# One fixed order for the first attention batch, and a first tile that takes 12 of its 16 weight slices

## The chip, the cores and the metric

One core of a Trainium2 chip runs the kernel. The metric is the device time of one execution in microseconds (us); lower is better. Engines go by the profile's names: PE is TensorE, DVE is VectorE, ACT is ScalarE, POOL is GpSimd, SP is SyncE, which here issues DMAs. PEld is PE's weight load.

## The reference

Eight batches of attention, 8 heads, 576 tokens, head width 64, whose keys and values are first averaged in groups of 8 tokens; then two feed-forward layers over all 4608 tokens, of width 512 and inner width 2048:

```
k_p, v_p = mean of 8 tokens of k, v
attn = softmax(q @ k_p.T / 8) @ v_p            # per batch and head
x = attn as (4608, 512)
x = leaky(x @ w_in1) @ w_out1                  # leaky(h) = max(0.01 h, h)
out = relu(x @ w_in2)**2 @ w_out2
```

The weights arrive as 64-bit floats, two 32-bit words a value.

## The kernel before, in words

Every product is made of three 32-bit ones: both operands are split into a high and a low part by a cast on ACT and a subtraction on DVE (`three`, lines 268 to 273).

**Layer 1, first way.** Tokens 0 to 2303 are cut into five tiles, `WIDE` = 512, 512, 512, 512, 256 (the last is the narrow tile). For a tile `t` and a weight slice `f` of 128 inner columns (16 slices), `first(t, f)` makes `h`, applies the leaky step, and splits it into `gh` and `gl` (L644 to L648); `second(t, f)` adds its product with the slice of `w_out` to four accumulators `acc`. A pair (t, f) is a unit: 24 matrix products. `units` holds the 80 pairs in order, and one loop walks them, with `split_weights` (L193, L194) two units and one unit ahead. At the last slice the accumulators are copied out (L676, L678) and stored into `x1`. The narrow tile's 256 columns make its products shorter.

**Layer 1, second way, and layer 2.** The other 2304 tokens (three passes) and all of layer 2 use a scheme with seven products in place of eight; its operands are prepared by `prepare_sums` (L214 to L218) and `prepare_products`.

**Decoding.** In the first pass over the slices each slice is fetched (two DMAs of 512 KB) and turned into 32-bit floats by `decode`: an absolute value on ACT (L159), a clip, a shift and a sign merge on DVE (L161, L164, L168), a conversion on ACT (L177) and an addition on DVE (L178). Two stage buffers hold fetched slices.

**Attention.** `attention` is a generator; the loop over units takes `RATES` steps of it per unit (3 in the first tile, 5 after). A batch is five chunks of up to 128 queries in two spans: `prepare_k` and `prepare_v` pool keys and values (L310), `stage_a` transposes queries (L452, L456), `stage_b` makes scores and their exponentials (L467, L475, L478, L487 to L499), `stage_c` transposes the weights, `stage_d` makes the output. For batch 0 the output goes straight into the first tile's `xh` and `xl` (L541, L542); later output goes to `x0` in memory and comes back by `load_x` and `split_x` (L622 to L629). Before the loop, steps of attention run until batch 0 is done, with a decode after every seventh step, up to `AHEAD` = 5 slices.

What sets the order: instructions are traced in program order, and a scheduler that ranks what is ready lays them out engine by engine. Each engine then runs its own list strictly in that order. All DMAs are issued from SP's queue.

Of the kernel before, what the change touches and what calls it, by code (L numbers as in the profile page):

```python
# [33 lines left out]
def attention_two_mlps(  # L34
# [25 lines left out]
    RATES = (3, 5)  # L60
# [5 lines left out]
    NTILE = len(WIDE)  # L66
    NQ = NF // 2
# [20 lines left out]

    def temp(name, dt=F32):
        return tpool.tile([P, TT], dt, tag="t", name=name)  # L90
# [14 lines left out]
    x0 += [dpool.tile([DM, HT], F32, name=f"x0_{NTILE + t}") for t in range(2 * LEAD)]  # L105
    x1 = [dpool.tile([DM, HT], F32, name=f"x1_{t}") for t in range(NT // HT)]
# [47 lines left out]
    def decode(st, r, name):  # L154
# [4 lines left out]
        nc.scalar.activation(raw(m), raw(high), AF.Abs)  # L159
# [19 lines left out]

    def decode_weights(f):  # L180
        r = (w_early if f < NQ else w_late).tile([P, 2, TT], U32, tag="w", name=f"w1_{f}")
        for _ in decode(RAW.pop(f), r, f"1_{f}"):
            pass
        W["in", f], W["out", f] = (raw(r[:, i]) for i in range(2))
# [91 lines left out]
    def attention():  # L276

        with ExitStack() as s:
# [42 lines left out]
            def load_main(b, src, nm, heads):  # L321


                ts = []
                for m in range(NP):
                    if m % 2 == 0:
                        ts.append(kv_tile(b, P, 2, f"{nm}{b}_{m}"))
                    for a in range(2):
                        nc.sync.dma_start(
                            out=ts[-1][a * KM:(a + 1) * KM, m % 2],  # L330
                            in_=src[b, heads[m][a], 0:KM * POOL, :].rearrange("(kk j) d -> kk (j d)", j=POOL),
                        )
                return ts

            def load_rest(b, src, nm):

                t = kv_tile(b, KR * H, 1, f"r{nm}{b}")
                nc.sync.dma_start(
# [8 lines left out]
            def load_k(b):  # L347
                if b < B:
                    KV["k", b] = (
                        load_rest(b, k, "k"),  # L350
                        load_main(b, k, "k", [[4 * (m // 2) + m % 2 + 2 * a for a in range(2)] for m in range(NP)]),
                    )
# [42 lines left out]
            def prepare_v(b):  # L395
# [10 lines left out]
                for g in range(2):  # L406
                    cols = slice(g * H * D // 2, (g + 1) * H * D // 2)
                    for j in range(3):
# [3 lines left out]
                        )  # L412
                for m in range(0, NP, 2):
# [5 lines left out]
                for a in range(2):  # L419
# [5 lines left out]
                    )  # L425
                flat = vR.rearrange("p m x -> p (m x)")
# [33 lines left out]
            def stage_b(b, span, at, off, n):  # L460
                qT = qt.pop((b, at))
                x = xp.tile([P, H, SP], F32, tag="x", name=f"x{b}_{at}", bufs=2)
                sm, rs = (xp.tile([P, H, 1], F32, tag=g, name=f"{g}{b}_{at}") for g in ("sm", "rs"))
                for e in range(2):
                    sc = work(f"s{b}_{at}_{e}", early=b == 0)[:, :H // 2 * SP].rearrange("p (h x) -> p h x", x=SP)
                    for m in range(2):
# [6 lines left out]
                    hs = slice(4 * e, 4 * e + 4)  # L473
                    mx = xp.tile([P, 4, 1], F32, tag="mx", name=f"mx{b}_{at}_{e}")
                    nc.vector.tensor_reduce(out=mx[:n], in_=sc[:n], axis=AX.X, op=ALU.max, negate=True)  # L475
                    if b < EARLY:
# [9 lines left out]
                if b >= EARLY:  # L486
                    nc.scalar.activation(x[:n], x[:n], AF.Exp)  # L487
                    nc.vector.tensor_reduce(out=sm[:n], in_=x[:n], axis=AX.X, op=ALU.add)
                nc.vector.tensor_scalar(out=sm[:n], in0=sm[:n], scalar1=1e-9, scalar2=None, op0=ALU.add)
# [15 lines left out]
            def stage_c(b, span, at, off, n):  # L505
                pp = pr.pop((b, at))
# [8 lines left out]
                yield  # L515
# [8 lines left out]
                )  # L524
                yield

            def stage_d(b, span):
                n = SPANS[span]
                g0 = b * S + sum(SPANS[:span])
                for m in range(NP):  # L530
# [7 lines left out]
                    if g0 < TT:  # L538
                        done = min(n, TT - g0)
                        xh, xl = X[1, 0][m]  # L540
                        nc.scalar.copy(xh[:, g0:g0 + done], o[:, :done])  # L541
                        nc.vector.tensor_tensor(  # L542
                            out=xl[:, g0:g0 + done], in0=o[:, :done], in1=raw(xh[:, g0:g0 + done]), op=ALU.subtract
                        )
                    if done < n:
                        xo = xp.tile([P, SPANS[0]], F32, tag="xo", name=f"xo{b}_{span}_{m}", bufs=3)
                        nc.scalar.copy(xo[:, done:n], o[:, done:n])
# [10 lines left out]
            pk, pv = prepare_k(0), prepare_v(0)  # L558
            load_k(0)
            load_q(*chunks[0])  # L560
            load_q(*chunks[1])
            yield
            load_v(0)
            yield from pk
            stage_a(*chunks[0])
            yield
            for i in range(len(chunks) + 1):
                if i < len(chunks):
                    b = chunks[i][0]
                    if i == nch - 2:  # L570
                        load_k(1)
                    if i % nch == nch - 1 and 0 < b < B - 1:
# [6 lines left out]
                    if i != nch:  # L579
                        stage_b(*chunks[i])  # L580
                        yield
                    if i == 0:
                        yield from pv
                    elif i % nch == 1 and b > 0:
                        yield from prepare_v(b)
                if i > 0:
                    b, span = chunks[i - 1][:2]
                    yield from stage_c(*chunks[i - 1])
                    if i == len(chunks) or chunks[i][:2] != (b, span):
                        yield from stage_d(b, span)  # L590
                    if i % nch == 0:
                        ready[0] = b + 1
                    if i == nch:

                        yield
                        yield from prepare_k(1)
                        stage_b(*chunks[nch])
                        yield

    ready = [0]  # L600
# [17 lines left out]
    def load_x(t):  # L618
        XS[t] = []
        for c in range(NK):  # L620
            st = temp(f"xs1_{t}_{c}")[:, :WIDE[t]]
            nc.sync.dma_start(out=st, in_=x0[t][c * P:(c + 1) * P, :])  # L622
# [30 lines left out]
    def store_x1(t, j, o):  # L653
        at = t * TT
# [7 lines left out]

    def second(t, f):
# [352 lines left out]
```

## Time and profile before

| what | value |
|---|---|
| median of 3 runs (lowest to highest) | 1664.58 us (1662.08 to 1665.07) |
| the profiled execution, its own time | 1663.77 us |
| its span | 1662.1 us |
| PE busy | 1610.6 us, 97% |
| PEld, DVE, ACT, POOL busy | 91%, 77%, 54%, 8% |
| PEclk in the first two of 40 slices (0 to 83 us), then | 0.7, 0.7, then 0.9 or more |
| DMA, mean | 241 GB/s |

The profiled execution's own time exceeds its span by 1.67 us, which lie around the program. PE's busy share is modelled: products overlap, and a waiting product can be counted as long. The span has three parts: up to 63 us attention's batch 0 with few of the large products; up to 598 us the five tiles with the other batches between them; then the seven-product scheme, where PE is busy throughout.

### The profile page before, as it was taken

What the parts mean: (1) busy time and instruction counts of PE and PEld (TensorE: products, weight loads), DVE (VectorE), ACT (ScalarE), POOL (GpSimd) and SP (SyncE); (2) the same over time, 40 slices, a digit from 0 to 9 for tenths busy, and PEclk for the clock granted to TensorE, in tenths of its full rate; (3) what the DMA queues carried; (4) which work ended last, traced back from release to release, by engine and by line L of the source; (5) the groups of instructions that cost most, each with busy time, mean ns of one, the idle gap of its engine ahead of it and who ended that gap; (6) DMA issues with size and microseconds to landing.
All of it is one profiled execution on the core that took longest, in us unless ns stands there. A gap on an engine that the chain in (4) does not pass through costs nothing.

```text
span 1662.1 us, 27194 instructions
## 1 busy us (share of the span) xinstructions
PE 1610.6 (97%) x9976; PEld 1518.0 (91%) x9976; DVE 1282.0 (77%) x1891; ACT 897.2 (54%) x1604; POOL 126.8 (8%) x149
## 2 busy tenths in 40 slices
PE   4899999999999999999999999999999999999998
PEld 3677788888888999999999999999999999999998
DVE  5899899888778989979979669378477486485484
ACT  5788655655657868668567425334234244244233
POOL 3131222232210000000000000000000000000000
PEclk7799999999999999999999999999999999999999
DMA  6565565866426769798887778878878879778776
GB/s 178 182 198 173 164 184 161 248 190 191 146 77 218 278 236 318 247 328 291 274 285 235 248 265 267 311 255 284 288 250 300 279 250 303 277 253 271 265 250 204
DMA packets 223717, 399.74 MB, mean 241 GB/s; under 512 B 56161, under 2 KB 129889, under 8 KB 223585
## 3 DMA queue, kind: packets, MB, share of 16 engines
q1 hardware_dynamic: 223584, 398.00, 73.1%
q8 instruction: 80, 1.31, 0.3%
q14 instruction: 53, 0.43, 0.1%
HBM read 318.77 MB, written 77.59 MB: 238 GB/s over the span
## 4 chain that ended last, share of the span: by engine, by line
PE 80%; DVE 11%; ACT 3%; DMA 3%; issue 2%; SPq 0%; POOL 0%; DVEq 0%; ACTq 0%; POOLq 0%
PE acc L273 13%; PE acc L272 13%; PE acc L271 13%; PE h L271 12%; PE h L273 12%; PE h L272 12%; PE s L467 2%; DVE hl_in L194 1%; DVE gl L648 1%; DMA st_in_out<-in_moe_w_out_dram 1%; DVE hl_out L194 1%; PE trq L452 1%; DVE v L310 1%; ACT x L478 1%; PE o L536 1%
## 5 line engine op out<-in xcount | busy, mean ns | idle before, releaser
L695 ACT CAST oh<-g 128x768 fp32r<-128x768 f32 x252 | 210.3, 835 | 261.4 <-PE acc L272 165.1
L271 PE MATMUL h<-xh,wb_in 128*128 128x384 f32 x1008 | 337.7, 335 | 2.5 <-ACT s L797 1.4
L273 PE MATMUL h<-xh,wb_in 128*128 128x384 f32 x1008 | 336.8, 334 | 0.0
L272 PE MATMUL h<-xl,wb_in 128*128 128x384 f32 x1008 | 336.8, 334 | 0.0
L696 DVE TENSOR_TENSOR ol<-g,oh 128x768 fp32r<-128x768 f32 x252 | 240.3, 954 | 77.5 <-ACT oh L695 76.9
L273 PE MATMUL acc<-wb_out,ol 128*128 128x256 f32 x1008 | 282.2, 280 | 0.0
L271 PE MATMUL acc<-wb_out,oh 128*128 128x256 f32 x1008 | 281.2, 279 | 0.0
L272 PE MATMUL acc<-wb_out,oh 128*128 128x256 f32 x1008 | 281.2, 279 | 0.0
L271 PEld LDWEIGHTS h<-xh,wb_in 128*128 128x128 f32 x1008 | 189.2, 188 | 5.0 <-ACT s L797 2.9
L272 PEld LDWEIGHTS acc<-wb_out,oh 128*128 128x128 f32 x1008 | 189.5, 188 | 0.0
L273 PEld LDWEIGHTS acc<-wb_out,ol 128*128 128x128 f32 x1008 | 189.2, 188 | 0.0
L272 PEld LDWEIGHTS h<-xl,wb_in 128*128 128x128 f32 x1008 | 189.2, 188 | 0.0
L273 PEld LDWEIGHTS h<-xh,wb_in 128*128 128x128 f32 x1008 | 189.2, 188 | 0.0
L271 PEld LDWEIGHTS acc<-wb_out,oh 128*128 128x128 f32 x1008 | 188.5, 187 | 0.0
L803 DVE TENSOR_TENSOR g<-h,s 128x768 f32<-128x768 f32 x36 | 34.4, 955 | 166.8 <-PE h L273 88.3
L699 DVE TENSOR_TENSOR g<-g,g 128x768 f32<-128x768 f32 x144 | 135.9, 953 | 1.0
L271 PE MATMUL h<-xh,hl_in 128*128 128x512 f32 (+1 forms) x320 | 122.8, 385 | 3.8 <-ACT x L478 1.9
L272 PE MATMUL acc<-gl,hl_out 128*128 128x512 f32 (+1 forms) x320 | 118.6, 373 | 2.0 <-DVE gl L648 2.0
L271 PE MATMUL acc<-gh,hl_out 128*128 128x512 f32 (+1 forms) x320 | 120.1, 384 | 0.1
L273 PE MATMUL acc<-gh,hl_out 128*128 128x512 f32 (+1 forms) x320 | 118.5, 373 | 1.7 <-DVE hl_out L194 1.7
L273 PE MATMUL h<-xh,hl_in 128*128 128x512 f32 (+1 forms) x320 | 119.8, 374 | 0.0
L272 PE MATMUL h<-xl,hl_in 128*128 128x512 f32 (+1 forms) x320 | 119.3, 373 | 0.0
(148 smaller groups left out, 3129.6 us busy)
## 6 DMA issues: line engine op xcount, KB each, us to landing
wb_in<-wd_in SPq DMA_DIRECT2D x204, 512.0 KB, 4.4
wb_out<-wd_out SPq DMA_DIRECT2D x204, 512.0 KB, 4.4
xs<-x SPq DMA_DIRECT2D x18, 768.0 KB, 5.2
wb_in<-ws_in SPq DMA_DIRECT2D x48, 256.0 KB, 3.7
wb_out<-ws_out SPq DMA_DIRECT2D x48, 256.0 KB, 2.8
out_dram<-o SPq DMA_DIRECT2D x24, 384.0 KB, 5.1
k<-in_k_dram SPq DMA_DIRECT2D x64, 128.0 KB, 2.7
q<-in_q_dram SPq DMA_DIRECT2D x32, 256.0 KB, 4.3
```

The costliest lines, as they stand in the source:

```text
L194: nc.vector.tensor_tensor(out=lo, in0=w, in1=raw(hi), op=ALU.subtract)
L271: nc.tensor.matmul(outp, ah, bh, start=first, stop=False, **kw)
L272: nc.tensor.matmul(outp, ah, bl, start=False, stop=False, **kw)
L273: nc.tensor.matmul(outp, al, bh, start=False, stop=last, **kw)
L310: nc.vector.tensor_tensor(out=dst if n == D else src[:, :, 0:n], in0=src[:, :, 0:n], in1=src[:, :, n:2 * n], op=ALU.add)
L452: nc.tensor.transpose(tr[:, m, :n], t[:n, 2 * m:2 * m + 2].rearrange("p a d -> p (a d)"), ident[:n, :n])
L467: nc.tensor.matmul(sc[:n, 2 * m:2 * m + 2].rearrange("p a x -> p (a x)"), qT[:, 2 * e + m, :n], kT[b % 2][:, 2 * e + m].rearrange("p a x - ...
L478: nc.scalar.activation(x[:n, 4 * e + h], sc[:n, h], AF.Exp, bias=mx[:n, h], accum_out=sm[:n, 4 * e + h],)
L695: nc.scalar.copy(hi, src)
L696: nc.vector.tensor_tensor(out=lo, in0=src, in1=raw(hi), op=ALU.subtract)
L699: nc.vector.tensor_tensor(out=out_, in0=a, in1=b, op=ALU.subtract)
L803: nc.vector.tensor_tensor(out=g11, in0=v, in1=s1, op=ALU.add)
```

## The change

- **One list.** `first_batch` traces the whole of batch 0, the decoding of slices 0, 1 and half of 2 and the first `first(0, 0)` as one sequence written out by hand. `in_order` ties each instruction of it to the one before it on the same engine, so the scheduler may not reorder it. `behind(marks[0], 3000)` keeps the next 3000 traced instructions behind the list on every engine.
- Half of batch 0's keys are loaded from ACT's queue; the values and all queries of the batch are queued ahead of slice 0, and batch 1's keys behind the list. For slices 0 and 1 the absolute value is a mask on DVE in place of ACT's.
- **Twelve of sixteen slices.** The first tile takes slices 0 to 11. Its partial sum goes to `y_first` in memory. A sixth tile, number 5, is the first one again with slices 12 to 15, behind the narrow tile; its input, stored in `x_first` as high and low part, comes back by a load from SP and an accumulating load from POOL; its output is added to `y_first`.
- Decoding runs at about 7 slices in 9 units in the first tile and at one in two units in the second, so slices 12 to 15 are decoded there. Attention takes 4 steps a unit in the first tile. `prepare_sums` starts once all 16 slices are there.

```diff
-    RATES = (3, 5)
+    RATES = (4, 5)
+    WIDE.append(TT)
+    CUT = 12
+    PART_OF = [range(CUT)] + [range(DFF // P)] * (NTILE - 1) + [range(CUT, DFF // P)]
...
+    def in_order(body):
+        traced = nc.cur_bb.bb.instructions
+        begin = len(traced)
+        body()
+        last = {}
+        for ins in traced[begin:]:
+            if ins.engine in last:
+                tc.add_manual_dep(
+                    ins, last[ins.engine].name,
+                    mybir.DependencyInfo(mybir.DependencyClass.NoSync, mybir.DependencyReason.DATA),
+                    reason="in_order",
+                )
+            last[ins.engine] = ins
+        return len(traced), last
...
-        nc.scalar.activation(raw(m), raw(high), AF.Abs)
+        if early:
+            nc.vector.tensor_scalar(out=m, in0=high, scalar1=0x7FFFFFFF, scalar2=None, op0=ALU.bitwise_and)
+        else:
+            nc.scalar.activation(raw(m), raw(high), AF.Abs)
...
+            def first_batch():
...
+                load_k(0)
+                q_in(0)
+                q_in(1)
+                load_v(0)
+                q_in(2)
...
+                w(1)
+                split_weights("in", 0, 1)
+                split_weights("out", 0, 0)
+                w(2)
+                w(2)
+                first(0, 0)
+                load_k(1)
+                w(2)
+                w(2)
+                a(5)
+                a(6)
+            marks.append(in_order(first_batch))
...
+            if t == NTILE:
+                nc.sync.dma_start(out=st, in_=x_first[0, c * P:(c + 1) * P, :])
+                nc.gpsimd.dma_start(out=st, in_=x_first[1, c * P:(c + 1) * P, :], accum_op=ALU.add)
...
+        if t == 0:
+            nc.sync.dma_start(out=y_first[j * P:(j + 1) * P, :], in_=o)
+            return
...
-        if f == NF - 1:
+        if t == NTILE and f == end - 1:
+            for j in range(4):
+                YF.append(temp(f"yf_{j}"))
+                nc.sync.dma_start(out=YF[j], in_=y_first[j * P:(j + 1) * P, :])
+        if f == end:
...
+                if t == NTILE:
+                    nc.vector.tensor_tensor(out=o, in0=acc[j], in1=YF[j], op=ALU.add)
...
-    units = [(t, f) for t in range(NTILE) for f in range(NF)]
+    units = [(t, f) for t in range(NTILE + 1) for f in PART_OF[t]]
...
-        if f == NF - 3 and t + 1 < NTILE:
+        if f == PART_OF[t][-1] - (2 if t + 1 < NTILE else 5) and t < NTILE:
...
-        if w1 < NF:
+        if w1 < (AHEAD + (i + 1) * (CUT - AHEAD) // (CUT - 3) if t == 0 else NF) and w1 < NF and (t == 0 or f % 2):
             prepare_weights(w1)
             w1 += 1
-        elif t > 0:
+        elif w1 == NF:
             next(sums1, None)
```

Three places show what moves. The first is DVE's list up to the first tile's first low part `gl_0_0`, before:

```order
L168 SCALAR_TENSOR_TENSOR wm_3_557<-st_in_out_553,wm_3_557 128x1024
L542 TENSOR_TENSOR xl_0_2_149<-o_1_2_626,xh_0_2_148 128x192
L178 ISA w_3_556<-wm_3_557,w_3_556 128x2048
L542 TENSOR_TENSOR xl_0_3_151<-o_1_3_635,xh_0_3_150 128x192
L194 TENSOR_TENSOR hl_in_2_695<-w_2_476,hl_in_2_695 128x512
L310 TENSOR_TENSOR rv_729<-rv_729 64x256
L161 TENSOR_SCALAR wm_4_619<-wm_4_619 128x1024
L310 TENSOR_TENSOR rv_729<-rv_729 64x128
L164 TENSOR_SCALAR wm_4_619<-wm_4_619 128x1024
L194 TENSOR_TENSOR hl_out_1_698<-w_1_362,hl_out_1_698 128x512
L168 SCALAR_TENSOR_TENSOR wm_4_619<-st_in_out_615,wm_4_619 128x1024
L648 TENSOR_TENSOR gl_0_0_670<-g_0_0_667,gh_0_0_669 128x512
```

and now (`wm` and `w` are a slice in decoding, `xl` the tile's low part, `rv` batch 1's values):

```order
L203 SCALAR_TENSOR_TENSOR wm_1_535<-st_in_out_270,wm_1_535 128x1024
L232 TENSOR_TENSOR hl_in_0_552<-w_0_344,hl_in_0_552 128x512
L612 TENSOR_TENSOR xl_0_0_147<-o_1_0_555,xh_0_0_146 128x192
L612 TENSOR_TENSOR xl_0_1_149<-o_1_1_565,xh_0_1_148 128x192
L612 TENSOR_TENSOR xl_0_2_151<-o_1_2_575,xh_0_2_150 128x192
L612 TENSOR_TENSOR xl_0_3_153<-o_1_3_585,xh_0_3_152 128x192
L213 ISA w_1_534<-wm_1_535,w_1_534 128x2048
L232 TENSOR_TENSOR hl_in_1_600<-w_1_534,hl_in_1_600 128x512
L232 TENSOR_TENSOR hl_out_0_603<-w_0_344,hl_out_0_603 128x512
L196 TENSOR_SCALAR wm_2_607<-wm_2_607 128x1024
L199 TENSOR_SCALAR wm_2_607<-wm_2_607 128x1024
L817 TENSOR_TENSOR gl_0_0_627<-g_0_0_624,gh_0_0_626 128x512
```

The first low part stood behind slices 0 to 3 and most of 4; now it stands behind slices 0 and 1 and half of 2, and none of batch 1's pooling is ahead of it. The second place is DVE's list at the start of the second tile, between the first tile's last copy and `gl1_1_1`, before:

```order
L194 TENSOR_TENSOR hl_out_1_1_2021<-w1_1_362,hl_out_1_1_2021 128x512
L512 TENSOR_TENSOR pt_l_181<-pt2_128_1992,pt_h_180 128x4x128
L310 TENSOR_TENSOR rd3_2506<-rv3_2204 64x64
L310 TENSOR_TENSOR vd3_2505<-v3_0_2206 128x128
L310 TENSOR_TENSOR v3_2_2211<-v3_2_2211 128x2x256
L217 TENSOR_TENSOR s1_in1_2452<-s1_in1_2452,w1_1_362 128x256
```

and now:

```order
L196 TENSOR_SCALAR wm_1_13_1828<-wm_1_13_1828 128x1024
L232 TENSOR_TENSOR hl_in_1_2_1854<-w1_2_606,hl_in_1_2_1854 128x512
L199 TENSOR_SCALAR wm_1_13_1828<-wm_1_13_1828 128x1024
L547 TENSOR_SCALAR sm2_256_1791<-sm2_256_1791 64x8
L232 TENSOR_TENSOR hl_out_1_1_1857<-w1_1_534,hl_out_1_1_1857 128x512
L548 RECIPROCAL rs2_256_1792<-sm2_256_1791 64x8
L203 SCALAR_TENSOR_TENSOR wm_1_13_1828<-st1_in13_out13_1824,wm_1_13_1828 128x1024
```

Slice 13 is decoded there, where a step of the sums stood. The third place is SP's queue in the narrow tile, where the operands of the seven-product scheme are fetched (`xs_0_0` and `xs_0_1` its input, `wb_in` its weights); now:

```order
L920 DMA wb_in_5_6252<-ws_in_138 128x512
L920 DMA wb_in_6_6254<-ws_in_138 128x512
L925 DMA wb_in_2_6256<-wd_in_122 128x1024
L920 DMA wb_in_7_6258<-ws_in_138 128x512
L788 DMA xs_5_0_6389<-x_first 128x512
L788 DMA xs_5_1_6392<-x_first 128x512
L788 DMA xs_5_2_6395<-x_first 128x512
L788 DMA xs_5_3_6398<-x_first 128x512
L920 DMA wb_in_3_6862<-ws_in_138 128x512
```

The four loads of the kept tile are new, between two weight blocks that stood next to each other; four accumulating loads follow them on POOL's queue.

## Rows read from the trace of the kernel before

**Rows 1.** Windows: window, length, busy us (instructions) by engine, PEclk, DMA share, GB/s.

```profile
0.00:63.00 63.00, 31.56 (x133) 26.64 (x133) 43.10 (x85) 36.66 (x127) 20.70 (x30) 0.72 0.64 174
63.00:71.10 8.10, 8.08 (x32) 6.47 (x33) 6.50 (x12) 5.60 (x13) 0.00 (x0) 0.90 0.51 141
71.10:187.70 116.60, 112.14 (x546) 90.35 (x546) 113.90 (x195) 92.11 (x243) 27.91 (x25) 0.99 0.66 193
187.70:322.30 134.60, 128.14 (x665) 105.26 (x665) 120.68 (x261) 76.50 (x195) 35.63 (x41) 0.97 0.61 178
322.30:449.00 126.70, 126.45 (x686) 106.08 (x685) 102.29 (x203) 74.27 (x157) 33.74 (x40) 1.00 0.63 188
...
550.60:600.00 49.40, 47.55 (x374) 45.87 (x373) 48.17 (x83) 39.95 (x82) 0.00 (x0) 1.00 0.66 229
```

**Rows 2.** Timeline, PE, 0 to 110 us: start, us, instruction, [idle before, releaser].

```profile
31.16 2.18 PE L467 MATMUL s<-kT,qT 128*64 128x144 f32 x8 [9.17 <-ACT qT L456]
...
59.48 0.58 PE L272 MATMUL o<-pt_l,vM 128*128 128x256 f32 x1 [4.14 <-DVE pt_l L512]
...
63.02 0.79 PE L271 MATMUL h<-xh,hl_in 128*128 128x512 f32 x1 [0.19 <-ACT xo L547]
...
88.36 0.39 PE L271 MATMUL h<-xh,hl_in 128*128 128x512 f32 x1
88.59 0.39 PE L272 MATMUL h<-xl,hl_in 128*128 128x512 f32 x1
```

**Rows 3.** Timeline, DVE, 0 to 112 us; same columns.

```profile
4.78 0.73 DVE L310 TENSOR_TENSOR rk<-rk 64x256 f32<-64x256 f32 x2 [4.78 <-DMA rk<-in_k_dram]
...
15.11 0.46 DVE L475 TENSOR_REDUCE mx<-s 128x4 f32<-128x288 f32 x1 [4.83 <-PE s L467]
...
54.66 0.69 DVE L161 TENSOR_SCALAR wm<-wm 128x1024 f32<-128x1024 f32 x1
55.39 0.69 DVE L164 TENSOR_SCALAR wm<-wm 128x1024 uint32<-128x1024 uint32 x1
56.11 1.22 DVE L168 SCALAR_TENSOR_TENSOR wm<-st_in_out,wm 128x1024 uint32<-128x1024 uint32 x1
57.48 1.23 DVE L178 CUSTOM_DVE_ANT_0 w<-wm,w 128x2048 uint16<-128x2048 uint16 x1
...
71.09 0.69 DVE L648 TENSOR_TENSOR gl<-g,gh 128x512 fp32r<-128x512 f32 x1
```

**Rows 4.** Lines by form, DVE, 0 to 200 us: count, busy us, mean ns, idle before.

```profile
L194 DVE TENSOR_TENSOR hl_in<-w,hl_in 128x512 fp32r<-128x512 f32 x20 | 16.7, 835 | 0.1
...
L648 DVE TENSOR_TENSOR gl<-g,gh 128x512 fp32r<-128x512 f32 x18 | 12.9, 714 | 0.0
...
L310 DVE TENSOR_TENSOR k<-k 128x512 f32<-128x512 f32 x8 | 5.5, 682 | 1.4 <-DMA k<-in_k_dram 1.3
...
L310 DVE TENSOR_TENSOR k<-k 128x256 f32<-128x256 f32 x8 | 3.3, 412 | 0.1
L310 DVE TENSOR_TENSOR kd<-k 128x128 f32<-128x128 f32 x8 | 3.0, 376 | 0.1
...
L218 DVE TENSOR_TENSOR s_out<-w,s_out 128x256 f32<-128x256 f32 x2 | 0.8, 418 | 0.0
```

**Rows 5.** Timeline, DVE, at the end of the second tile.

```profile
321.63 0.69 DVE L678 COPY o<-acc 128x512 f32<-128x512 f32 x1 [0.67 <-PE acc L273]
```

**Rows 6.** Timeline, SP's queue, 0 to 95 us.

```profile
1.67 4.99 SPq L329 DMA_DIRECT2D k<-in_k_dram  x8
...
7.96 0.83 SPq L146 DMA_DIRECT2D st_in_out<-in_moe_w_in_dram  x1
```

**Rows 7.** DMA issues: count, KB each, median us from issue to landing.

```profile
xs<-x SPq DMA_DIRECT2D x12, 256.0 KB, 2.8
```

**Rows 8.** Timeline, POOL, 0 to 95 us.

```profile
19.95 1.55 POOL L499 TENSOR_TENSOR p<-x,rs 128x96 f32<-128x96 f32 x2
...
88.47 3.88 POOL L499 TENSOR_TENSOR p<-x,rs 128x96 f32<-128x96 f32 x2
```

More of the change, by code (lines that the diff above doesn't have):

```diff
@@ L87, in attention_two_mlps, with behind @@
     mpool = ctx.enter_context(tc.tile_pool(name="m", bufs=1, side="right"))
+    def in_order(body):
[12 more added lines that the diff above has]
+        return len(traced), last
+    def behind(mark, n):
+        traced, (end, last) = nc.cur_bb.bb.instructions, mark
+        for ins in traced[end:end + n]:
+            if ins.engine in last:
+                tc.add_manual_dep(
+                    ins, last[ins.engine].name,
+                    mybir.DependencyInfo(mybir.DependencyClass.NoSync, mybir.DependencyReason.DATA),
+                    reason="behind",
+                )
     def temp(name, dt=F32):
@@ L178, in decode, with decode_steps @@
             nc.vector.tensor_tensor(out=r, in0=m, in1=r, op=ALU.add)
+    def decode_steps(f):
+        r = (w_early if f < NQ else w_late).tile([P, 2, TT], U32, tag="w", name=f"w1_{f}")
+        yield from decode(RAW.pop(f), r, f"1_{f}", early=f < 2)
+        W["in", f], W["out", f] = (raw(r[:, i]) for i in range(2))
     def decode_weights(f):
-        r = (w_early if f < NQ else w_late).tile([P, 2, TT], U32, tag="w", name=f"w1_{f}")
-        for _ in decode(RAW.pop(f), r, f"1_{f}"):
+        for _ in decode_steps(f):
             pass
-        W["in", f], W["out", f] = (raw(r[:, i]) for i in range(2))
     HL = {}
@@ L541, in stage_d @@
                         nc.scalar.copy(xh[:, g0:g0 + done], o[:, :done])
+                    if done < n:
+                        xo = xp.tile([P, SPANS[0]], F32, tag="xo", name=f"xo{b}_{span}_{m}", bufs=3)
+                        nc.scalar.copy(xo[:, done:n], o[:, done:n])
+                    if done:
                         nc.vector.tensor_tensor(
@@ L889, in attention_two_mlps @@
     new_x(0)
-    step, w1 = 0, 0
-    while ready[0] < 1:
-        next(att)
-        step += 1
-        if step == 1:
-            RAW[0] = fetch_weights(1, [("in", 0), ("out", 0)])
-        if step % 7 == 0 and w1 < AHEAD:
-            prepare_weights(w1)
-            w1 += 1
+    next(att)
+    w1 = 3
     while w1 < AHEAD:
@@ L903, in attention_two_mlps @@
     put_stores(made)
+    for c in range(NK):
+        for i in range(2):
+            later(4 + 2 * c, out=x_first[i, c * P:(c + 1) * P, :], in_=raw(X[1, 0][c][i]))
     at_work, due = True, 0
@@ L925, in attention_two_mlps @@
             load_x(t + 1)
-        if f == NF - 1 and t + 1 < NTILE:
+        if f == PART_OF[t][-1] and t < NTILE:
             split_x(t + 1)
```

207 lines of the change are left out of this document (152 added, 55 removed).

## The prediction

> **What bounds the kernel now.** I read the windows first, then PE's and DVE's timelines of the first 110 us, then DVE's groups by form. The reader is to see four stretches [rows 1]. Up to 63.0 us PE is busy for 31.56 us of 63, at a granted clock of 0.72, between the levels of 1.2 and 2.4 GHz. From 71.1 to 187.7 us, the rest of the first tile, DVE is busy for 113.90 of 116.60 us and PE for 112.14: both are full. In the second tile, to 322.3 us, DVE has 120.68 of 134.60. From 322.3 us on PE has 126.45 of 126.70 and DVE has room. So PE bounds the program from the third tile on, and what happens before is worth what it moves the end of the second tile.
>
> In PE's timeline [rows 2] the first product of the first tile starts at 63.02 us. Ahead of it PE waits 9.17 us for a query transpose that had stood behind other work, and 4.14 us for DVE's `pt_l`, which stood behind the decoding of a slice. A warm 512-column product takes 0.23 us (88.36 to 88.59), so a unit of 24 takes 5.5 us. DVE's timeline [rows 3] shows that decoding, 54.66 to 58.7: 0.69 + 0.69 + 1.22 + 1.23 = 3.83 us of DVE a slice. The first low part `gl` runs at 71.09. I follow DVE from there, because it is the engine that stays full, and PE's loss follows from it.
>
> **The start.** Up to 71.1 us DVE is busy for 43.10 + 6.50 = 49.6 us and idle for 21.5 [rows 1]. The new list takes out of this stretch:
> - decoding: slices 0 to 3 and three steps of slice 4 (4 x 3.83 + 2.6 = 17.9) become slices 0 and 1, two masks of 0.69 (taken from the clip, the same size) and two steps of slice 2 (7.7 + 1.4 + 1.4 = 10.4): 7.5 us less;
> - splits of two weight parts (three `hl_in` and two `hl_out` become two and one), at 0.7 each: 1.4 less [rows 4];
> - batch 1's pooling of keys, 2 x (0.68 + 0.41 + 0.38) = 2.9, and six or seven small ones that I put at 1.5 from their length: 4.4 less [rows 4].
>
> That leaves 49.6 - 13.3 = 36.3 us busy. Of the idle 21.5 the first 4.78 us, until the first keys land, stay [rows 3]. The wait for the first scores, 4.83 us, is partly filled: value pooling now stands in it, and half of the keys come from a second queue, which saves half of eight issues that took 4.99 us [rows 6]; I keep 3. Of the other 11.9 I keep half, since exponentials still have to end before sums, and slice 0, issued at 7.96 before [rows 6], now queues behind all values and three more chunks of queries. That is 14 us idle, and the first `gl` at 50.3 us, 20.8 earlier. Ends: 10 us idle (46.3) and no idle saved (57.8). The first product then starts near 44.
>
> **The first two tiles.** From the first `gl` to the second tile's last copy, which waits 0.67 us for PE and starts at 321.63 [rows 5], DVE was busy for 113.90 + 120.68 = 234.6 us and idle for 16.6 [rows 1]. The change puts here what it took from the start: 8.9 of decoding (the 7.5 above is net of the two masks, which are new work of 1.4 for DVE) and 4.4 of pooling. Four units are gone: four `gl` and, with what was done ahead, three `hl_in` and three `hl_out`, 10 x 0.78 = 7.8 less [rows 4]. Ten steps of the sums at 0.42 move to the third tile: 4.2 less [rows 4]. Together 8.9 + 4.4 - 7.8 - 4.2 = +1.3, so 235.9 us. DVE is now the bound for the whole stretch: PE has 28 units, 154 us, and the batches' products, some 24 us a tile by what the first window leaves beside 16 units (112.14 - 88.3). What stays open is DVE's idle time. No row shows a stretch where DVE alone is the bound; the ends are 0 and the 16.6 us of before. I take 8: the first tile's 2.7, and five of the second tile's 13.9, since a fuller list hides more of its waits. So the second tile ends at 50.3 + 235.9 + 8 = 294.2 us against 322.3: 28.1 us earlier (ends 40 and 12).
>
> **The four units behind the narrow tile** cost PE 96 x 0.23 = 22.1 us. They were in the first tile, where they had their share of a window that both engines filled. In the balance the saved 28.1 is left with 6.0.
>
> **Third tile.** The 4.2 us of sums fall where DVE has 24 us of room [rows 1]; cost 0, and 4.2 if that cover were gone.
>
> **Narrow tile.** DVE is busy for 48.17 of 49.40 us there [rows 1]. By its list it gets four `xl` of the kept tile and four more `hl_in` and `hl_out`, 5.5 us, and loses 3.5 us of preparation that moves behind it: +2.0, uncovered (ends 0 and 4).
>
> **The kept tile's load.** Four loads of 256 KB on SP and four accumulating ones behind them on POOL, asked for five narrow units, 15 us, before the tile. A plain load of this size lands after 2.8 us [rows 7]; no row shows an accumulating one. Lower end 2.8 + 2.8, hidden. Upper end: POOL's pair of multiplications took 1.55 us early and 3.88 us at 88.47, when DVE ran without a pause [rows 8]; four loads one after another, stretched 2.5 times, are 2.8 + 4 x 7 = 30.8 us, 15 too many. I take 0, since the nearest row is the plain load. ACT's cast of the first part stands between two units' casts, so a late load would stop the narrow tile's last units too.
>
> **The rest.** Four additions of the stored part (0.69 each, 2.8 us) take the place of copies shared by ACT and DVE; the next products write other banks: 0, at most 2.8. Twelve stores of 256 KB and twelve loads lie on DMA engines that are 60 to 66% busy [rows 1] and on a queue that nobody waits for at those points: 0.
>
> **Sum.** -28.1 + 22.1 + 2.0 = -4.0 us. The profiled execution took 1663.77 us (span 1662.1, and 1.67 around it), so 1659.8; the median of the runs is 0.8 above it, 1664.58. I say 1660.
>
> **Rivals.**
> - *DVE hardly waits.* The start ends at 47 and the two tiles keep 2 us of waits, as in the first tile before. For it: a list written by hand can put each instruction where its operands are ready, and DVE had 97.7% in the first tile. Against it: PE is no longer full, so DVE must wait for products more often. 1659.8 - 3.5 - 6 = 1650.
> - *DVE waits as before.* All 16.6 us stay, and the start ends at 55 because slice 0 and the rounds of exponentials come late. For it: in the first tile PE has 12 units and 24 us of attention, 90 of some 106 us, where it had 96%; the granted clock was 0.72 in the one stretch where PE was much less busy [rows 1], products then take longer, and `gl` waits for them. 1659.8 + 4.7 + 8.6 = 1673, slower. It turns slower at 12 us of waits with the start as forecast.
> - *The kept tile comes late*, slower too. The place is the narrow tile's end; it decides if the last accumulating load lands over 15 us after it was asked for. From the 2.5-fold stretch of POOL beside a full DVE: up to 15 us, 1666 to 1675, middle 1670. The Trainium skill's page "SBUF — State Buffer", section "SBUF: two separate sides", states this as a rule: a DMA issued from GpSimd needs GpSimd to write its descriptors, and some VectorE instructions lock it out. By that rule the four loads stretch and 1670 is the time; by the landing row it is 1660. Against it: POOL has nothing else to do there.
>
> **Chances.** A measurement of this kernel tells about 0.2%, 3.3 us, from no change, so faster is below 1661.25. The forecast (1654 to 1667, the end of the second tile moving by 6 us) gets 0.45: 0.25 of it faster, 0.19 the same, 0.01 slower. Hardly waiting: 0.22, all faster. Waits as before: 0.20, of it 0.04 the same. Late load: 0.13, of it 0.02 the same. Together 0.47, 0.25, 0.28. The range takes in both sides, 1648 to 1675.
>
> **What would show it.** Right: the first product near 44 us and the first `gl` near 50; DVE over 95% busy and PE near 85% in the first tile; the second tile's last copy near 294; `xs` of the kept tile landed before its cast. Wrong: the first `gl` after 55; DVE idle for over 12 us between it and that copy; PE waiting for `xh` at the narrow tile's end; or a last copy before 287, where the gain would be twice what I say.

## The result, and the profile after

The change made the kernel slower: 1672.91 us (1667.88 to 1676.57, 8 runs) against 1663.62 us (1660.76 to 1667.13, 8 runs), a ratio of 1.0055 with an interval of 1.0045 to 1.0065, or 9.2 us at 1663. The prediction said 1660 and a gain of 4. In the profiled execution (span 1671.0 us against 1662.1) the windows of the change read as follows; columns as in [rows 1].

```profile
0.00:47.40 47.40, 25.00 (x125) 20.76 (x125) 30.04 (x67) 27.46 (x119) 16.45 (x30) 0.90 0.68 162
47.40:53.50 6.10, 6.07 (x23) 4.99 (x24) 4.59 (x9) 3.94 (x7) 0.00 (x0) 0.69 0.78 219
53.50:168.20 114.70, 97.62 (x464) 78.30 (x463) 102.79 (x175) 86.62 (x235) 24.05 (x25) 0.93 0.71 205
168.20:306.40 138.20, 130.17 (x670) 106.18 (x670) 131.45 (x281) 80.98 (x203) 40.23 (x41) 0.98 0.63 182
306.40:534.10 227.70, 226.81 (x1178) 189.44 (x1178) 185.49 (x356) 140.76 (x277) 42.33 (x53) 1.00 0.59 185
534.10:585.40 51.30, 50.03 (x386) 47.70 (x385) 49.61 (x86) 42.25 (x89) 3.69 (x4) 1.00 0.74 242
585.40:1670.90 1085.50, 1075.59 (x7138) 1069.77 (x7136) 780.14 (x936) 512.74 (x683) 0.00 (x0) 1.00 0.82 271
```

The boundaries are the first product, the first `gl`, the last output copies of the first, second and fourth tile, and the narrow tile's. The first product, in PE's timeline, starts 15.6 us earlier than in [rows 2]:

```profile
47.43 0.79 PE L309 MATMUL h<-xh,hl_in 128*128 128x512 f32 x1 [1.03 <-DVE xl L612]
```

DVE's timeline has the first `gl` at 53.50 us, 17.6 earlier than in [rows 3], and the second tile's last copy at 305.74, 15.9 earlier than in [rows 5]:

```profile
53.50 0.69 DVE L817 TENSOR_TENSOR gl<-g,gh 128x512 fp32r<-128x512 f32 x1 [0.51 <-ACT gh L816]
...
305.74 0.69 DVE L860 COPY o<-acc 128x512 f32<-128x512 f32 x1
```

What follows that copy takes 24.8 us more than before: 1671.0 - 306.4 against 1662.1 - 322.3. So -15.9 + 24.8 = +8.9, the difference of the spans.

PE's busy time is the same in both kernels, 1610.6 and 1611.3 us, so the loss is, but for 0.7 us, idle time of PE. From the windows, length less busy time, with the two halves of the change from the first experiment beside it:

| PE idle, us | before | list alone | cut alone | the change |
|---|---|---|---|---|
| to the first `gl` | 31.5 | 21.9 | 32.3 | 22.4 |
| rest of the first tile | 4.5 | 11.9 | 10.7 | 17.1 |
| second tile | 6.5 | 4.9 | 6.5 | 8.0 |
| everything behind | 9.0 | 11.6 | 12.4 | 12.2 |
| sum | 51.5 | 50.3 | 61.8 | 59.7 |

The start gave 9.1 us, the first tile took back 12.6. DVE tells why: before the first `gl` it now does 34.6 us of work where it did 49.6 [rows 1], but what it did not do there it does behind: the first two tiles hold 102.79 + 131.45 = 234.2 us of DVE work for four units fewer. It waits there for many things, each a little. Waits of the change from 53.5 to 305.7 us, DVE's and then PE's, as total, times and longest:

```profile
DVE mx L528 <- PE s L518: 5.4, 4, 1.8
DVE gl L817 <- ACT gh L816: 4.3, 6, 1.5
DVE sm L547 <- ACT x L535: 2.4, 4, 1.0
DVE hl_in L232 <- ACT hl_in L231: 1.6, 2, 0.9
```

```profile
PE h L309 <- ACT hl_in L231: 4.6, 1, 4.6
PE h L309 <- DVE x L540: 3.8, 2, 2.7
PE o L309 <- ACT pt_h L569: 3.5, 2, 3.0
PE acc L309 <- ACT hl_out L231: 2.3, 2, 1.3
```

DVE waits for PE and ACT, and PE for ACT and DVE. DVE's four lines add up to 13.7 of its 18.7 idle us, and none of these waits is longer than 1.8 us: a ring of short waits, not one late operand.

### The profile page after: what moved, and what is told of

Read it like the earlier page. It is cut to its first block, busy times and chain, and to the rows that moved or that the text cites. A ratio compares the mean times of both kernels' runs of the same rounds, so it can differ in the third digit from the quotient of the medians.

```text
span 1671.0 us, 27261 instructions
## 1 busy us (share of the span) xinstructions
PE 1611.3 (96%) x9976; PEld 1517.1 (91%) x9976; DVE 1284.1 (77%) x1901; ACT 894.8 (54%) x1606; POOL 126.8 (8%) x153
## 4 chain that ended last, share of the span: by engine, by line
PE 60%; DMA 2%; DVE 2%; ACT 1%; issue 0%; SPq 0%; DVEq 0%; ACTq 0%
PE acc L311 10%; PE acc L310 10%; PE acc L309 10%; PE h L309 10%; PE h L310 10%; PE h L311 10%; DMA wb_in<-ws_in 1%; DMA wd_in<-hl_in 0%; DMA wd_out<-hl_out 0%; DMA yf<-y_first 0%; DMA wb_out<-wd_out 0%; ACT s L979 0%; DVE hl_out L296 0%; DVE wb_in L932 0%; ACT g L952 0%
## 5 line engine op out<-in xcount | busy, mean ns | idle before, releaser
L309 PE MATMUL h<-xh,hl_in 128*128 128x512 f32 (+1 forms) x320 | 125.1, 391 | 9.7 <-ACT hl_in L231 4.9
L311 PE MATMUL h<-xh,hl_in 128*128 128x512 f32 (+1 forms) x320 | 121.1, 378 | 0.0
```

The source lines that it names most:

```text
L309: nc.tensor.matmul(outp, ah, bh, start=first, stop=False, **kw)
L311: nc.tensor.matmul(outp, al, bh, start=False, stop=last, **kw)
```

## Experiments

Each kernel is timed against the kernel before on the same chip; ratios carry a 95% interval. A difference to the change is the difference of two such ratios, times 1663 us. "DVE idle" is counted from 0 to the start of the second tile's last copy.

### The two halves

`list_only` undoes the cut, `cut_only` is the kernel before with the cut, the kept tile, the slower decoding and the rates of 4 and 5 steps. Of the first one's edit:

```diff
-    RATES = (4, 5)
+    RATES = (3, 5)
...
-    WIDE.append(TT)
-    CUT = 12
-    PART_OF = [range(CUT)] + [range(DFF // P)] * (NTILE - 1) + [range(CUT, DFF // P)]
+    PART_OF = [range(DFF // P)] * NTILE
...
```

Expected of the list alone:

> The list of fixed order alone: the first tile keeps its 16 slices, nothing is put behind the narrow tile, rates and decode pace as before the change. Theory A (VectorE bounds the first two tiles, and the list only shifts its idle time): VectorE's work up to the second tile's end stays at some 284 us and its idle time near 37, so 1660 to 1665 us, within 4 us of the kernel before. Theory B (the list gains what the start shows, 15.6 us earlier first products, and the cut to 12 slices gives it back): 1645 to 1652. Theory C (the fixed order costs, the cut would gain): 1668 or more.

Expected of the cut alone:

> The cut alone: 12 slices in the first tile, four units behind the narrow tile, the slower decode pace and the rates of 4 and 5 steps, with the start of the kernel before. Theory A: four units' work of VectorE, some 13 to 16 us, leaves the first two tiles and 24.8 us come in behind the narrow tile, so 1672 to 1678 us, 9 to 14 above the kernel before. Theory B: about the same, as the cut alone carries the loss: 1675 to 1685. Theory C: 1660 or less.

Measured: list alone 1662.3 us, ratio 0.9998 (0.9989 to 1.0008); cut alone 1677.39 us, 1.0086 (1.0073 to 1.0099). Both lie in theory A's ranges, the cut alone near the upper end. Theory B (the list gains, the cut gives back) and theory C (the fixed order costs) fall with the list alone. Windows of the list alone, its first tile and the whole to the second tile's end:

```profile
52.80:185.10 132.30, 120.39 (x554) 94.08 (x553) 124.79 (x213) 100.55 (x255) 34.17 (x25) 0.95 0.64 188
...
0.00:316.70 316.70, 278.01 (x1371) 224.04 (x1371) 279.61 (x550) 208.38 (x574) 85.81 (x96) 0.96 0.64 183
```

The first `gl` comes 18 us earlier than before, yet the first tile ends only 1.8 us earlier (185.1 against 186.9): DVE is busy for 124.79 us in it against 113.90 [rows 1], since decoding and pooling of keys moved in. The cut alone, to the start of the second tile's last copy, and the kernel before to the same point:

```profile
0.00:308.80 308.80, 259.35 (x1279) 210.36 (x1280) 270.54 (x528) 201.83 (x562) 87.87 (x96) 0.95 0.63 187
```

```profile
0.00:321.60 321.60, 279.21 (x1371) 228.27 (x1371) 283.50 (x547) 210.44 (x575) 84.24 (x96) 0.93 0.63 182
```

The cut ends this stretch 12.8 us earlier. The four units are 22.1 us of PE work behind the narrow tile, but the cut frees DVE of 13.0 us only (283.5 to 270.5), eight steps of the sums that move behind the second tile included. DVE idle is 38.1 us before, 37.1 with the list, 38.3 with the cut, 37.5 with both. In these four kernels the end of the second tile followed DVE's busy time. Within the stretch the idle time moved: in the cut alone the first tile holds 11.4 us of it (2.7 before), at a granted clock of 0.97:

```profile
70.50:172.20 101.70, 91.05 (x445) 72.90 (x446) 90.26 (x154) 77.68 (x222) 24.36 (x25) 0.97 0.70 209
```

### The rule that keeps later work behind the list

```diff
-        if i == NF:
-            behind(marks[0], 3000)
```

> The change without the one rule that holds the next 3000 instructions behind the list's last one of each engine. Theory A: later work may slip into the list's gaps, a few us at most: 1668 to 1674 us. Theory C (the fixed order costs): under 1666.

Measured: 1674.03 us, 1.0065 (1.0052 to 1.0078), the change's own 1.0055 within its interval. In the change the rule costs nothing that can be told, and theory C fails here too.

### Does DVE's amount of work set the time?

Two kernels take the 1.34 us merge out of the decoding of slices 3 to 15, or do it twice; two more leave out ScalarE's scaled copy, alone and with the merge, and change two constants so that the weights stay finite. Of their edits:

```diff
-        nc.vector.scalar_tensor_tensor(
-            out=m, in0=high, scalar=0xC0000000, in1=m, op0=ALU.bitwise_and, op1=ALU.bitwise_or
-        )
+        for _ in range(merges):
+            nc.vector.scalar_tensor_tensor(
+                out=m, in0=high, scalar=0xC0000000, in1=m, op0=ALU.bitwise_and, op1=ALU.bitwise_or
+            )
...
-            nc.scalar.activation(r, low, AF.Copy, scale=2.0 ** -29)
-            nc.vector.tensor_tensor(out=r, in0=m, in1=r, op=ALU.add)
+            if whole:
+                nc.scalar.activation(r, low, AF.Copy, scale=2.0 ** -29)
+            nc.vector.tensor_tensor(out=r, in0=m, in1=r if whole else m, op=ALU.add)
```

Once less:

> The change without VectorE's merge of sign and top exponent bit (1.34 us each) when slices 3 to 15 are decoded; that step of the decoding is left out, so those weights have other values. It takes 13 x 1.34 = 17.4 us of VectorE's work out of the first two tiles. In the four kernels so far the end of the second tile was VectorE's busy time plus 37.1 to 38.3 us. Theory A (that sum holds: VectorE bounds, its idle time stays): the second tile ends 14 to 17.4 us earlier, total 1655 to 1660 us. Theory D (the engines wait for each other and for TensorE at its lower clock, VectorE's load decides little): under 6 us, 1667 or more.

Twice:

> The change with that same merge done twice for slices 3 to 15: 17.4 us more of VectorE's work in the first two tiles. Theory A: the second tile ends 15 to 18 us later, total 1688 to 1691 us. Theory D: the 18.7 us of VectorE's idle time there take up most of it: under 1680.

Without the scaled copy:

> The change without ScalarE's scaled copy of the low words (1.17 us each) in the decoding of slices 3 to 15, and with constants that keep the weights finite; the low words are left out of those weights, so they have other values. It takes 13 x 1.17 = 15.2 us of ScalarE's work out of the first two tiles and none of VectorE's. Taking 17.4 us from VectorE gave only 6.5, so something lies right beneath it. Theory A (VectorE, then TensorE's own waits): within 3 us of the change, 1670 to 1675. Theory E (ScalarE's link of the decoding is that something): some 3 to 6 us below, 1667 to 1670, as VectorE is still there.

Without both:

> Both left out for slices 3 to 15: VectorE's merge (17.4 us) and ScalarE's scaled copy (15.2 us); those weights have other values. Theory E: with both engines relieved the first two tiles gain what VectorE's work alone should have given, 14 to 18 us: 1655 to 1659. Theory A: little below the run without the merge alone: 1663 to 1667.

| kernel | us | ratio to before | to the change, us |
|---|---|---|---|
| merge twice | 1688.05 | 1.0141 (1.0122 to 1.0160) | +14 |
| no merge | 1666.37 | 1.0018 (1.0006 to 1.0031) | -6 |
| no scaled copy | 1673.15 | 1.0058 (1.0042 to 1.0074) | 0 |
| neither | 1662.69 | 0.9999 (0.9988 to 1.0009) | -9 |

The run with the merge twice is theory A's, at the lower end of its range. The 17.4 us were an estimate: DVE's group of merges grew by 14.3 us (21.2 to 35.5), the second tile's last copy came 14.0 later (319.7 against 305.7) and the program took 14 more. The run without the merge is a miss for both theories, 0.6 us below theory D's range: 17.5 us of merges went, DVE's busy time to that copy fell by 14.6, and the copy came only 7.7 earlier, as DVE idle rose to 44.4 us. First-tile windows, of the merge twice, of no merge, and of neither:

```profile
52.50:179.90 127.40, 102.12 (x456) 78.65 (x455) 115.91 (x188) 87.08 (x235) 25.88 (x25) 0.89 0.69 196
```

```profile
53.70:162.50 108.80, 97.97 (x465) 78.91 (x465) 92.79 (x166) 85.30 (x233) 25.85 (x25) 0.92 0.74 212
```

```profile
52.90:156.90 104.00, 92.02 (x453) 73.77 (x451) 90.67 (x165) 75.19 (x222) 24.34 (x25) 0.97 0.74 220
```

Against the change's 102.79 us of DVE work in 114.7: 13.1 us more work made this tile 12.7 longer; 10.0 less made it 5.9 shorter, and DVE idled more; 12.1 less, with ScalarE's copies gone too, made it 10.7 shorter. The scaled copy alone is worth nothing that can be told, as theory A had it. So DVE's work bounds this stretch as it stands: more of it costs its full length. Less of it returns about half, so another limit lies right beneath. Theory E takes ScalarE's link of the decoding for it. That isn't shown: without both the time is 3 us below the run without the merge, but the two intervals touch (0.9988 to 1.0009 and 1.0006 to 1.0031), part of it is DVE's own 2.1 us less in the first tile, and 1662.69 lies 0.3 below theory A's range and 3.7 above theory E's.

### The pace of decoding, and what SP's queue holds up

```diff
-        if w1 < (AHEAD + (i + 1) * (CUT - AHEAD) // (CUT - 3) if t == 0 else NF) and w1 < NF and (t == 0 or f % 2):
+        if w1 < (min(AHEAD + i + 1, CUT) if t == 0 else NF) and w1 < NF and (t == 0 or f % 2):
```

> The change with one slice decoded per unit of the first tile, up to the twelfth, instead of seven per nine units. If its units wait because their slice is decoded too late (ScalarE waited 11.2 us in the first two tiles for a decoded slice before it split it), 3 to 6 us below the change: 1667 to 1670. If VectorE's amount of work decides and not its order: 1671 to 1675.

Measured: 1678.08 us, 1.0092 (1.0077 to 1.0107), 6 us above the change and outside both ranges. Its first tile ends at 162.0 us, 6.2 before the change's, as the first theory had it, and then the second tile takes 146.5 us. DVE's longest wait in that tile, and SP's two longest from 205 to 256 us:

```profile
DVE k L348 <- DMA k<-in_k_dram: 9.6, 2, 9.0
```

```profile
SPq L491 <- PE s L518: 10.1, 1, 10.1
SPq L450 <- POOL rv L442: 9.0, 1, 9.0
```

The next batch's keys (L367) are issued on SP behind a load of queries that waits for a buffer PE still reads (L491) and behind copies of `rx` that wait for GpSimd (L450). Two kernels issue these copies behind the key loads, and a third from GpSimd's queue (`nc.gpsimd.dma_start` for every batch but the first). Of the first two's edit, which also takes the copies out of their old place for these batches:

```diff
...
                 if b > 0:
                     load_k(b + 1)
+                    for g in range(2):
+                        cols = slice(g * H * D // 2, (g + 1) * H * D // 2)
+                        for j in range(3):
+                            nc.sync.dma_start(
...
```

The faster pace with it:

> One slice decoded per unit of the first tile, and the six rx copies of a batch (which wait for GpSimd's rv) issued behind the next batch's key loads instead of ahead of them on SP's queue. Theory F (the pace of decoding delays the first tile by 6 us, and the loss of the run with the faster pace was the one key load behind those copies): the second tile ends near 300 us, total 1665 to 1668. If the faster pace only shifts idle time from the first tile to the second: 1671 or more.

The change with it, at its own pace:

> The change with the six rx copies of a batch issued behind the next batch's key loads, nothing else. VectorE waited for no key load in the change's first two tiles, so Theory F: within 3 us of the change, 1670 to 1676. If SP's queue is behind more of the idle time than the waits show: 1668 or less.

The faster pace with the copies on GpSimd's queue:

> One slice decoded per unit of the first tile, and the rx copies issued from GpSimd's own queue, so that SP never waits for GpSimd. Theory F: as the copies behind the key loads, 1665 to 1668. If issuing six copies a batch on GpSimd holds up its products p, or slows VectorE as GpSimd's subtraction did: 1671 or more.

Measured: 1671.29 us, 1.0056 (1.0043 to 1.0068); 1669.72, 1.0046 (1.0033 to 1.0059); 1672.61, 1.0065 (1.0047 to 1.0083). Theory F falls: freeing the queue took the faster pace's extra loss away, but it ends level with the change. With the copies behind the key loads its first tile still ends 3 us earlier (165.2 against 168.2), its second at 304.7 against 305.7, in a profiled execution of 1674.87 us, above its median. So the faster pace mostly shifts idle time from one tile to the next, and no single link of the ring was found that could be taken out. In the change itself the freed queue is worth 1.5 us in the median, which the intervals don't tell from nothing, though DVE idle fell from 37.5 to 34.6 us in its profile, and from 37.1 to 32.6 in the list alone's (below): some of the waits hang on that queue.

### The kept tile's load

```diff
-        if f == PART_OF[t][-1] - (2 if t + 1 < NTILE else 5) and t < NTILE:
+        if f == PART_OF[t][-1] - (2 if t + 1 < NTILE else 9) and t < NTILE:
```

Nine units ahead:

> The change with the kept tile's input asked for four units earlier (nine units ahead of the narrow tile's last instead of five). Theory A: its accumulating transfers land in time either way, but for one wait of 2.0 us: 1671 to 1674 us. The rival that the kept tile comes late: 5 us or more below the change.

Three units ahead:

> The change with the kept tile's input asked for three units ahead of the narrow tile's last instead of five. Asked for nine units ahead, the narrow tile took 59.0 us instead of 51.3. If the four of six staging buffers that the waiting input holds are what stretches it, two units less give 1 to 4 us: 1669 to 1672. If its landing (6.6 to 8.5 us) decides, it now comes late for the kept tile's first product: 1674 to 1680.

Measured: 1680.99 us, 1.0110 (1.0095 to 1.0125), and 1673.37, 1.0059 (1.0047 to 1.0072). Asking later changes nothing; asking earlier costs 9 us, which no theory had. ACT's waits and PE's in the narrow tile of the earlier one:

```profile
ACT xh L797 <- DMA xs<-x_first: 7.3, 1, 7.3
```

```profile
PE acc L309 <- ACT gh L816: 5.6, 1, 5.6
```

The earlier request also moved ACT's first cast of the kept input forward in ACT's list: ACT came to it at 555.6 us instead of 569.2, and 7.3 us ahead of the landing. ACT stood, a unit's `gh` stood behind it, and the narrow tile took 59.0 us instead of 51.3, at a granted clock of 0.94 instead of 1.00. So the place that the prediction's third rival names can cost this much, in an experiment and not in the change, and by the cast's place and not by GpSimd: its issues took 1.0 to 1.9 us each here too. The theory about staging buffers is not borne out.

### Looking for a version that gains

Four edits to the list alone, in five kernels. Fewer attention steps in the second tile, more in the third:

```diff
-    RATES = (3, 5)
+    RATES = (3, 4, 6, 5)
...
-        rate = RATES[min(t, 1)]
+        rate = RATES[min(t, 3)]
```

> The list alone, with the attention's steps spread otherwise: four steps a unit in the second tile where it had five, six in the third where it had five. Theory A: VectorE's work leaves the second tile, where it is the bound, for the third, where it was busy 104 of 126 us: the second tile ends 8 us or more earlier, of which the third gives a part back, as TensorE is busy through it: 1654 to 1660 us. Theory D: 1661 to 1664, no difference.

Low parts of the output-side slices of the first tile on GpSimd:

```diff
-        nc.vector.tensor_tensor(out=lo, in0=w, in1=raw(hi), op=ALU.subtract)
+        split = nc.gpsimd if kind == "out" and t == 0 else nc.vector
+        split.tensor_tensor(out=lo, in0=w, in1=raw(hi), op=ALU.subtract)
```

> The list alone, with the low part of each output-side weight slice of the first tile subtracted on GpSimd instead of VectorE: 16 x 0.71 = 11.4 us less for VectorE there. At the rate of the run without the merge (6.5 us for 17.4), 4 us: 1657 to 1660 us, below the kernel before. If GpSimd's own order or its slower subtraction makes TensorE wait: 1663 or more.

The `rx` copies behind the key loads; the same with the new rates; the same without `behind`:

> The list alone with the six rx copies of a batch behind the next batch's key loads. Theory F: no key load was waited for there either; 1660 to 1664 us. If SP's queue matters: 1655 to 1659, below both kernels.

> The list alone, the rx copies behind the key loads, and the rates of 3, 4, 6 and 5 steps a unit. If the two edits' effects add (1660.9 and 1662.0 beside 1662.3 for the list alone): 1659 to 1661 us, just below the kernel before. If TensorE, busy through the third tile, takes it all back: 1661 to 1663.

> The list alone with the rx copies behind the key loads and without the rule that holds later instructions behind the list. In the change that rule moved nothing that could be measured (1674.0 without, 1672.9 with): 1660 to 1663. If it keeps useful work out of the list's gaps: 1656 to 1659.

| list alone, with | us | ratio to before |
|---|---|---|
| rates 3, 4, 6, 5 | 1661.99 | 0.9994 (0.9985 to 1.0004) |
| GpSimd's subtraction | 1670.93 | 1.0050 (1.0035 to 1.0064) |
| `rx` behind | 1660.91 | 0.9990 (0.9981 to 1.0000) |
| `rx` behind, the rates | 1663.39 | 1.0002 (0.9991 to 1.0013) |
| `rx` behind, no `behind` | 1658.93 | 0.9977 (0.9966 to 0.9987) |

The first is in theory D's range, the second in the rival's of its expectation; the `rx` copies alone are in theory F's, with the rates 0.4 us above both ranges, and without `behind` in that of "keeps useful work out". The rates are a miss for theory A that teaches. Windows to the second tile's end, and of the third tile:

```profile
0.00:307.30 307.30, 269.00 (x1320) 216.45 (x1321) 272.16 (x529) 204.04 (x562) 81.74 (x90) 0.96 0.65 187
307.30:442.90 135.60, 133.68 (x732) 111.25 (x731) 106.11 (x223) 77.61 (x166) 34.52 (x46) 1.00 0.62 184
```

The second tile ends 9.4 us before the list's 316.7, but 9.0 us of PE work (278.0 to 269.0) went with the steps. The third tile, full for PE, ends at 442.9, where the list alone ended it at 442.6. So moving work that PE has to do all the same wins nothing; only its idle time is there to be won.

The last kernel is faster than both by a little, 0.23% below before. Its first tile:

```profile
53.70:181.20 127.50, 114.50 (x554) 89.60 (x552) 124.73 (x215) 99.75 (x254) 35.63 (x25) 1.00 0.69 198
```

DVE does the same work as in the list alone (124.73 us). PE, though idle for 13.0 us, kept a granted clock of 1.00 where the list alone had 0.95, so its products took 114.50 us instead of 120.39. That doesn't show where the gain comes from: this execution took 1661.21 us, above its median, and its second tile ends at 313.9 us, as with the `rx` copies alone (314.4). The intervals of these two kernels overlap. In the change `behind` cost nothing, so its removal here is not a rule.

## Why the prediction was wrong

- **The start.** Forecast: DVE busy 36.3, idle 14, first `gl` at 50.3. Measured: 34.6, 18.9, 53.5, inside its ends (46.3 to 57.8). Idle fell by 2.6 in all, from 21.5. The wait for the first scores nearly went, but DVE now waits 2.36 us for the first values and 2.59 for slice 0, so the half of the 11.9 us of waits that was to go did not.
- **The first two tiles, DVE's work.** Forecast 235.9, measured 234.2. Right.
- **The first two tiles, DVE's idle time: the step that failed.** "I take 8 ... since a fuller list hides more of its waits", between ends of 0 and 16.6. It was 252.9 - 234.2 = 18.7, outside both ends. By stretch, with the two halves of the change:

| DVE idle, us | before | forecast | list alone | cut alone | the change |
|---|---|---|---|---|---|
| to the first `gl` | 21.5 | 14 | 18.1 | 21.0 | 18.9 |
| rest of the first tile | 2.7 | 2.7 | 7.5 | 11.4 | 11.9 |
| second tile | 13.9 | 5 | 11.5 | 5.9 | 6.8 |
| sum | 38.1 | 22 | 37.1 | 38.3 | 37.5 |

  The second tile's 5 was nearly right. The first tile's 2.7, taken over from the kernel before, was not: it was 11.9 in a tile where PE had 12 units beside the same attention, was busy for 85% (as forecast, but 97.6 us of 114.7 instead of 90 of 106), and DVE for 90%, not 95%. The reasoning treated idle time as something that fuller work fills. In these four kernels its sum hardly moved, only its place: the list carries some of it from the start into the first tile, the cut from the second tile into the first.
- **PE's room.** "Some 24 us a tile" for the batches' products holds for the first tile only; for the second, [rows 1] leave 128.14 - 88.3 = 39.8. PE was busy for 227.8 us of the two tiles, not the 202 that the prediction adds up, and in the second tile it is as full (130.17 of 138.20) as DVE (131.45). So DVE was not alone as the bound of the whole stretch.
- **The sum.** +3.2 from the start, -1.7 from the work, +10.7 from the idle time: the second tile ended at 306.4 instead of 294.2, 15.9 us earlier instead of 28.1. That is the error but for 0.7.
- **The four units and the narrow tile.** Forecast 22.1 + 2.0, measured 24.8 for everything behind the second tile; the narrow tile took 1.9 more (51.3 against 49.4). Right.
- **The kept tile's load.** Forecast 0. ACT waited for it once (who waited for tile `xs`, total and times):

```profile
  ACT xh L797: 2.0, 1
```

  PE's waits in the narrow tile were 0.7 us and less. The forecast came true by luck: the landings were not those of [rows 7] (below). Asked for from 555.4 us on, the first accumulating load landed at 571.2, and the last, issued at 566.5, at 573 to 575 by the landing times of these loads (an estimate), 18 to 20 us after the request. That is past the 15 us that the prediction gives them. It did no harm because the kept tile's first product came at 579.6, 24 us after the request. The Trainium skill's page "SBUF — State Buffer", section "SBUF: two separate sides", would have GpSimd locked out of writing descriptors during some VectorE instructions. GpSimd's four issues took 1.0 to 1.8 us each, and only that one cast waited, so the 1670 of that rule had no part in the result.
- **The rivals.** "DVE waits as before" was the case. Its reason is borne out in part: PE was no longer full, at a granted clock of 0.93 in the first tile, `mx` waited for PE, and `gl` for ACT's `gh`, while ACT waited 27.2 us for PE's `h`. But the cut alone has nearly the same idle time in that tile at 0.97, with waits for exponentials and a key load at the top of its list, so the lower clock isn't needed for it. The rival's 1673 is what was measured, with the start at 53.5 instead of 55 and 18.7 us idle instead of 16.6. Its stated point (slower from 12 us of waits on) was passed. It had 0.20, and the evidence for more stood in [rows 1]: DVE lost 13.9 of 134.6 us in the second tile, with PE, the busier of the two (128.14), short of full as well. (In the first rival 50.3 to 47 is 3.3 us, not 3.5; nothing hangs on it.)

What stays open is why the 18.7 us are there. Pace, SP's queue and DVE's load each moved some of it (from the program's start DVE idle ranges from 32.6 to 44.4 us over all runs), and none is shown to be the cause alone. A hand-written order for the first two tiles, as the list is for the first batch, wasn't tried.

## What to carry to other kernels

Here an engine that was some 90% busy, in a ring of engines that wait for each other, kept the sum of its idle time when its work was reordered and when units were taken out (37.1 to 38.3 us in four kernels). So price such idle time at what it was, summed over the whole stretch and not tile by tile, and lower it only if a run shows that it falls. Starting earlier by putting work off gained nothing here, as the engine that did the work is the bound behind, too. And units taken out of a stretch were worth there what they freed of its bounding engine (13 us of DVE), while behind they cost what they take of the engine that bounds the place they go to (22 us of PE).

## What the hardware showed

GpSimd slowed DVE by more than it relieved it. Rows of DVE's groups by form in the first tile (53 to 185 us), list alone and then with GpSimd's subtraction, and GpSimd's own:

```profile
L201 DVE SCALAR_TENSOR_TENSOR wm<-st_in_out,wm 128x1024 uint32<-128x1024 uint32 x14 | 17.0, 1215 | 0.0
...
L230 DVE TENSOR_TENSOR hl_in<-w,hl_in 128x512 fp32r<-128x512 f32 x17 | 12.5, 734 | 0.6 <-ACT hl_in L229 0.5
```

```profile
L201 DVE SCALAR_TENSOR_TENSOR wm<-st_in_out,wm 128x1024 uint32<-128x1024 uint32 x14 | 19.2, 1373 | 0.1
...
L231 DVE TENSOR_TENSOR hl_in<-w,hl_in 128x512 fp32r<-128x512 f32 x16 | 16.7, 1043 | 0.4 <-ACT hl_in L229 0.4
```

```profile
L231 POOL TENSOR_TENSOR hl_out<-w,hl_out 128x512 fp32r<-128x512 f32 x15 | 28.2, 1880 | 61.9 <-ACT hl_out L229 33.4 <-PE trq L496 9.7 <-PE o L601 7.8
```

A subtraction that DVE does in 0.69 us took GpSimd 1.88 us in the mean and 1.44 in the median, and DVE's other work stretched: `hl_in` from 0.73 to 1.04 us, the merge from 1.22 to 1.37. The stretch lies where the two meet: the five `hl_in` that began 0.2 to 0.6 us after one of GpSimd's subtractions took 1.52 to 1.77 us, ten of the other eleven 0.67 to 0.69. Sixteen subtractions, 11 us, left DVE, yet its busy time to the second tile's end rose from 279.6 to 285.9 us. The same section of the Trainium skill's page has GpSimd and two-input instructions of VectorE take turns at one pair of ports, each for a whole instruction; the stretch agrees.

The kept tile's loads landed after 8.5 us (plain) and 7.5 us (accumulating), where a load of that size took 2.8 us elsewhere [rows 7]. DMA issues of the change, 555 to 600 us: count, KB, median us to landing:

```profile
xs<-x_first SPq DMA_DIRECT2D x4, 256.0 KB, 8.5
xs<-x_first POOLq DMA_DIRECT2D x4, 256.0 KB, 7.5
```

The plain one is as late as the accumulating one, so the delay goes with this stretch of the program and not with the accumulation: the DMA share is 0.74 in the narrow tile here, 0.66 before [rows 1]. That the share is the cause isn't shown.
